# Two load queues instead of one: value loads of units 1 to 15 issued by ScalarE in a decode attention kernel

## The chip, the core and the metric

The kernel runs on one core of a Trainium2 chip. The metric is the device time of one execution in microseconds. The kernel before has a median of 440.01 us over 3 runs (439.67 to 440.44).

## What is computed

Two attention blocks, A and B, each decode one token for a batch of 4. Both have 32 query heads, 8 key/value heads, head size 128 and a cache of 8192 keys. Block A attends to all keys, block B to the last 2048 (`W`). The outputs lie side by side in one array of 4 x 1 x 1024.

```python
q = (x @ wq) -> (B, 32, 1, 128)          # x is 4 x 1 x 512
k, v = caches, each of 8 heads repeated 4 times
scores = einsum("bhqd,bhkd->bhqk", q, k) * 128 ** -0.5
p = softmax(scores)
out = einsum("bhqk,bhkd->bhqd", p, v) -> (B, 1, 4096) @ wo
# block A: keys 0..8191; block B: keys 6144..8191
```

The caches that are read are large and each value is used for one token only: 20 units, below, of 4 MiB of keys and 4 MiB of values, with 8 MiB of query weights and 8 MiB of output weights.

## The kernel before, in words

**Units and turns.** The work is cut into 20 units. Units 0 to 3 belong to block B: one batch element each, all 8 heads, 2048 keys. Units 4 to 19 belong to block A: two key/value heads of one batch element, all 8192 keys. Each unit has 4 MiB of keys (`K_sb`) and 4 MiB of values (`V_sb`), and each buffer has two slots, taken by even and odd units in turn. Two units make a turn; TensorE runs a hardware loop over ten turns, VectorE and ScalarE over the last seven (`emit_loop`), with the first three turns written out.

**TensorE, in one unit u.** Sixteen transpose jobs T0 to T15 (L279, four 128x128 transposes each of keys) go into four PSUM banks in rotation. Three jobs behind follow the scores S (L310). Even jobs are copied from PSUM to `KT_sb` by VectorE (L287), odd ones by ScalarE (L288). After the last transposes come the sums of the exponentials of unit u-1 (L338), a filler in even units or the output projection in odd ones (L384, `Wo_sb`), and 128 matmuls PV of probabilities and values of unit u-1 (L326). So unit u's keys are needed at its beginning, and its values only near the end of unit u+1.

**VectorE** finishes unit u-1 after PV with a small sum and a product (L489, L492); this last one is the event `otr`, and it frees the value slot of unit u-1. At the end of an odd unit VectorE adds the projection's result to `oacc` (L392), the event `ocp`. **ScalarE** has, per unit, eight copies L288 (jobs 1, 3, ... 15) and two exponentials (L457), in this order.

**Loads.** All large loads are issued by SyncE (SP), in one hand-written order: both query weights (into the value slots), keys of unit 0, and then for u = 1 to 20: keys of unit u, values of unit u-1, and in front of units 6, 8, ... 18 also a 1 MiB piece of the output weights `Wo_sb` for the turn that starts (behind the values of unit u-1). Block B's loads are four DMAs of 1 MiB each per unit and kind, block A's one of 4 MiB. The function is `kv_load`, and the helper that issues every DMA is at L568. What each waits for, in SP's own order, so that a later one never goes ahead of an earlier one that waits:

- keys of unit u: up to unit 5 the transposes of unit u-2 that free the slot; from unit 6 on `otr` of unit u-3, which comes at the end of unit u-2, after PV.
- values of unit u: `otr` of unit u-2, at the end of unit u-1.
- output weights of a turn: `ocp` of the turn before, at the end of its odd unit.

```python
w = [("otr", u - 2)] if kind == "V" else [("otr", u - 3)] if u >= 2 * T0P else [("T", tjob_idx[(u - 2, NJ - 1)])]
```

Block A's loads are preceded by a semaphore addition of 48 on the same engine, so that loads of 16 and of 4 x 16 counts look alike to the loops.

The values of unit 19 come in five pieces, followed by eight small pieces of output weights (`Wl_sb`), for a short end.

Of the kernel before, what the change touches and what calls it, by code (L numbers as in the profile page):

```python
# [14 lines left out]
def bass_concat_heads__gqa_block_cached__sliding_block_cached__decode_kernel(  # L15
# [16 lines left out]
    _, HKV, SK, DH = A_k_cache.shape  # L32
    HQ = A_wq.shape[1] // DH
    REP = HQ // HKV
    W = min(4096, max(256, SK // 4))
    assert DH == 128 and D % 128 == 0 and D <= 512
    DC = D // 128
    NT = SK // 64
    NSEG = 4
# [7 lines left out]
    NQP = 4  # L47
# [4 lines left out]
    NM = 128  # L52
    NBK = 4
    NFILL = 3
    NTH = NT // 2
    X = [A_x, B_x]
    KC = [A_k_cache, B_k_cache]
# [14 lines left out]
    with ExitStack() as es:  # L72
# [93 lines left out]
        def op(eng, fn, waits=(), inc=None, bump=None):  # L166
            waits = list(waits)
            if not (eng == "pe" and turn[0] is not None):
                waits = [w for w in waits if w is not None]
            t = turn[0] if eng == "pe" or (eng in ("dve", "act") and turn[0] is not None and turn[0] >= T0P) else None  # L170
            plan[eng].append(dict(fn=fn, waits=waits, inc=inc, turn=t, bump=bump))

        def add(d):
            op(d["eng"], d["fn"], waits=d["waits"], inc=d["inc"])
# [426 lines left out]
        assert pc == NC  # L601
        AFTER = {("S", 2): ("OT",), ("S", 5): ("OL",)}

        for u in range(NU):
            turn[0] = tn = u // 2
            odd = u % 2 == 0
            ev = {}
            extra = {}
            at = -1

            def anchored(d):
                extra.setdefault(at, []).append(d)
            for tok in TOK:
                if tok[0] == "T":
                    ev[tok[1]] = pe_T(u, tok[1])
                    if tok[1] % 2 == 0:
                        at = tok[1]
                elif tok[0] == "S":
                    pe_S(u, tok[1])
                elif tok[0] == "X":  # L620
                    if u % 2 == 1:
                        ev["opj"] = pe_job_OPJ(tn)
                    else:
                        pe_filler(NFILL)
                elif tok[0] == "SM":
                    pe_SM(u - 1)
                else:
                    pe_PV(u - 1, tok[1], waits=[("V", u - 1) if u >= 1 else None] if tok[1] == 0 else [])
                if odd and tok in AFTER:
                    kind = AFTER[tok][0]  # L630
                    anchored({"OT": pe_job_OT, "OL": pe_job_OL}[kind](tn))

            if u % 2 == 0 and tn:
                follow[opj_idx[tn - 1]] = tjob_idx[(u, 0)]
            for k in range(0, NJ, 2):
                add(ev[k])
                if k == 10:
                    add(dve_max(u, 0))
                for d in extra.get(k, []):
                    add(d)  # L640
            add(dve_max(u, 1))
            if units[u]["P"] == 0:
                add(dve_maxc(u))
            add(dve_addmask(u))
            if u >= 1:
                add(dve_sum(u - 1))
                add(dve_rcp(u - 1))
            add(dve_submask(u))
            add(dve_sub(u, 0))
            add(dve_sub(u, 1))  # L650
            if u >= 1:
                add_norm(u - 1)
            if u % 2 == 1:
                add(ev["opj"])

            for k in range(1, NJ, 2):
                add(ev[k])
            add(act_exp(u, 0, 1))
            add(act_exp(u, 1, 2))

            if u % 2 == 0:
                if tn:
                    op("pool", None, waits=[("ocp", tn - 1)])
                if tn - 1 == T0P + NSEG - 1:
                    op("pool", lambda pool: pool.tensor_copy(out=osb[:, 1, :], in_=oacc[:, :]), inc=("ocB", 0))
                    op("pool", lambda pool: pool.memset(oacc[:, :], 0.0), waits=[("ocB", 0)], inc=("ocB", 1))
                add(pool_otp(tn))
            if u + 1 < NU:
                add(pool_rq(u + 1))
            add(pool_ar1(u))  # L670
            if u >= 1 and units[u - 1]["P"] == 0:
                add(pool_oc(u - 1))
# [34 lines left out]
        op("act", lambda act: act.activation(out=osb[:, 0, H2:D], in_=halves[1], func=ACTF.Copy), waits=[("fin", 1)], inc=("Ef",))  # L707
        op("act", dma(out[:, 0, H2:D], osb[:, 0, H2:D]), waits=[("Ef",)], inc=("out", 2))

        def kv_load(kind, u):  # L710
            un = units[u]
            cache = (KC if kind == "K" else VC)[un["P"]]
            buf = K_sb if kind == "K" else V_sb
            slot = u % 2
            if kind == "K" and slot == 1 and u < L:
                op("sp", lambda sp: sp.sem_inc(sems["kh"], 16), bump=(sems["kh"], 16, ("KH", u)))
            if un["P"] == 1:
                for q in range(NSEG):
                    base = cache[un["b"], 2 * q, SK - W:SK, :]
                    src = bass.AP(tensor=base.tensor, offset=base.offset, ap=[[TS * DH, 64], [SK * DH, 2], [1, TS * DH]])  # L720
                    if kind == "K":
                        w = [("T", tjob_idx[(u - 2, 4 * q + 3)])] if u >= 2 else []
                    else:
                        w = [("otr", u - 2)] if u >= 2 else [("T", tjob_idx[(1, 1)])] if u else [("T", qp_idx[(1, NQP - 1)])]
                    op("sp", dma(buf[:, slot, q * TS:(q + 1) * TS, :], src), waits=w, inc=(kind if q == NSEG - 1 else kind + "h", u, q))
                return
            base = cache[un["b"], 2 * un["gp"], :, :]
            w = [("otr", u - 2)] if kind == "V" else [("otr", u - 3)] if u >= 2 * T0P else [("T", tjob_idx[(u - 2, NJ - 1)])]
            if kind == "V" and u == L:
                c0 = 0  # L730
                for i, n in enumerate(VCH):
                    t0, t1 = c0 * TC, (c0 + n) * TC
                    src = bass.AP(tensor=base.tensor, offset=base.offset + t0 * DH, ap=[[NT * DH, 128], [1, (t1 - t0) * DH]])
                    op("sp", dma(buf[:, slot, t0:t1, :].rearrange("p t d -> p (t d)"), src), waits=w, inc=("VL", i))
                    c0 += n
                return
            src = bass.AP(tensor=base.tensor, offset=base.offset, ap=[[NT * DH, 128], [1, NT * DH]])
            sem = sem_of((kind, u))
            op("sp", lambda sp: sp.sem_inc(sem, 48), waits=w, bump=(sem, 48, None))
            if kind == "K" and u == L:  # L740
                for h in range(2):
                    t0 = h * NTH
                    src = bass.AP(tensor=base.tensor, offset=base.offset + t0 * DH, ap=[[NT * DH, 128], [1, NTH * DH]])
                    op("sp", dma(buf[:, slot, t0:t0 + NTH, :].rearrange("p t d -> p (t d)"), src), inc=(kind, u, 0) if h == 0 else ("KH", u))
                return
            op("sp", dma(buf[:, slot, :, :].rearrange("p t d -> p (t d)"), src), inc=(kind, u, 0))

        for P in (1, 0):
            op("sp", dma(V_sb[:, 1 - P, :, :].rearrange("p t d -> p (t d)"), WQ[P].rearrange("(p c) n -> p (c n)", p=128)), inc=("WQ", P))
        kv_load("K", 0)  # L750
        for u in range(1, NU + 1):
            if u < NU:
                kv_load("K", u)
            kv_load("V", u - 1)
            tn = u // 2
            if u % 2 == 0 and tn in pieces:
                P, q = pieces[tn]
                src = WO[P][q * C * DH:(q + 1) * C * DH, :].rearrange("(p r) n -> p (r n)", p=128)
                op("sp", dma(Wo_sb[:, :, :].rearrange("p r n -> p (r n)"), src), waits=[("ocp", tn - 1)], inc=("wo", tn))
            if u == 16:  # L760
                op("sp", dma(out[:, 0, D:2 * D], osb[:, 1, :]), waits=[("ocB", 0)], inc=("out", 1))
# [14 lines left out]

        values = {}
        counters = {}
        for eng in plan:
            for o in plan[eng]:  # L780
                if o["bump"] is not None:
                    sem, amt, key = o["bump"]
                    counters[sem.name] = counters.get(sem.name, 0) + amt
                    if key is not None:
                        values[key] = (sem, counters[sem.name], amt)
                if o["inc"] is not None:
                    key = o["inc"]
                    sem = sem_of(key)
                    amt = 16 if key[0] in DMA_KEYS else 1
                    counters[sem.name] = counters.get(sem.name, 0) + amt  # L790
                    assert key not in values, key
                    values[key] = (sem, counters[sem.name], amt)
# [102 lines left out]

        @block.scalar
        def _(act):
            emit_loop("act", act, mybir.EngineType.Activation)

        @block.vector  # L900
        def _(dve):
# [33 lines left out]
```

## Time and profile before

| What | Value |
|---|---|
| Median of 3 runs | 440.01 us (439.67 to 440.44) |
| The profiled execution, its own time | 439.76 us |
| Its span in the trace | 437.9 us, so 1.9 us lie around it |
| Granted TensorE clock | 0.969 of full speed |
| Busy: TensorE, VectorE, ScalarE, GpSimd | 363.9, 209.5, 193.3, 29.1 us |
| Read from memory | 184.56 MB, 421 GB/s over the span |
| TensorE waits for block A's keys | 33.0 us, 10 times |

How to read it. The page has the busy time of each engine, the span in 40 slices with the DMA engines' share and rate, the DMA queues, and groups of instructions by line. A timeline lists an engine's instructions in order of time: start, busy time, engine, line, operation, and in square brackets the idle time before it with what ended it. The rows of SPq are the DMA issues of SyncE's instruction stream; POOLq and ACTq those of GpSimd and ScalarE. A row of DMA issues gives the count, the size of one, and the median time from issue to landing; asked for a short window, it gives this for a single load.

### The profile page before, as it was taken

The numbers are of one execution on the slowest core, as the hardware profiler recorded it, in microseconds if no ns is written. First come the engines' busy times: TensorE is split into PE (matmuls) and PEld (weight loads), VectorE is DVE, ScalarE is ACT, GpSimd is POOL, SyncE is SP. The second block draws the span as 40 slices with busy tenths as digits, with TensorE's granted clock in tenths as the row PEclk, the third lists the DMA queues.
The fourth block names the chain that finished last, engine by engine and source line by source line (L and its number), as shares of the span: only waits on it lengthen the run. The fifth ranks groups of instructions, "written<-read, shape, count | busy, mean of one in ns | idle before, by whom it ended". The sixth has DMA issues, their size and how long they took to land.

```text
span 437.9 us, 15510 instructions
## 1 busy us (share of the span) xinstructions
PE 363.9 (83%) x7174; PEld 336.5 (77%) x7184; DVE 209.5 (48%) x404; ACT 193.3 (44%) x217; POOL 29.1 (7%) x96
## 2 busy tenths in 40 slices
PE   0078898998998959896989598969878895989986
PEld 0068897997997959795979588968868795979975
DVE  0004455664565634463456247625644563556641
ACT  1033473563653625372635264534534361635630
POOL 7110000000000000000000000000100000000000
PEclk9999999999999997999899699989998999999999
DMA  8999999999999999999999999999999999999996
GB/s 336 431 412 418 419 419 419 421 445 406 450 431 431 417 445 431 434 428 431 434 434 428 432 434 431 428 434 431 406 456 431 431 428 434 431 431 410 446 407 253
DMA packets 12500, 184.75 MB, mean 422 GB/s; under 512 B 1428, under 2 KB 2504, under 8 KB 2760
## 3 DMA queue, kind: packets, MB, share of 16 engines
q1 hardware_dynamic: 12400, 184.56, 99.2%
q8 instruction: 8, 0.13, 0.1%
q14 instruction: 4, 0.03, 0.0%
q0 software_dynamic: 64, 0.02, 0.0%
q10 hardware_dynamic: 24, 0.01, 0.0%
HBM read 184.56 MB, written 0.01 MB: 421 GB/s over the span
## 4 chain that ended last, share of the span: by engine, by line
PE 51%; DMA 43%; issue 2%; DVE 1%; SPq 1%; PEld 1%; PEldq 0%
DMA K_sb<-in_A_k_cache_dram 29%; PE KT L279 25%; PE OT L326 10%; DMA K_sb<-in_B_k_cache_dram 7%; DMA V_sb<-in_A_v_cache_dram 7%; PE SB L310 4%; PE SA L310 4%; PE KT L384 4%; SPq L568 1%; PE SA L338 1%; DVE oacc L392 1%; PE KT L326 1%; PEld OT L326 1%; PE KT L262 0%; DVE OS L489 0%
## 5 line engine op out<-in xcount | busy, mean ns | idle before, releaser
L279 PE MATMUL KT<-identf,K_sb 128*128 128x128 f32 x1280 | 206.2, 294 | 44.0 <-DMA K_sb<-in_A_k_cache_dram 33.0
L288 ACT ACTIVATE KT_sb<-KT 128x1024 bf16<-128x1024 bf16 x160 | 163.4, 1025 | 121.1 <-PE KT L279 121.1
L279 PEld LDWEIGHTS KT<-identf,K_sb 128*128 128x128 f32 x1280 | 146.2, 148 | 49.4 <-DMA K_sb<-in_A_k_cache_dram 34.2
L287 DVE COPY KT_sb<-KT 128x512 int32<-128x512 int32 x160 | 110.5, 690 | 131.2 <-PE KT L279 129.9
L326 PE MATMUL OT<-PT,V_sb 128*128 128x64 bf16 x2560 | 78.1, 193 | 2.5 <-issue 1.4
L326 PEld LDWEIGHTS OT<-PT,V_sb 128*128 128x128 bf16 x2560 | 75.9, 98 | 2.7 <-issue 1.5
L457 ACT ACTIVATE PT<-Dt 128x512 bf16<-128x512 f32 x40 | 24.6, 632 | 84.1 <-DVE Dt L446 84.1
L310 PEld LDWEIGHTS SA<-RQc,KT_sb 128*128 128x128 bf16 x1280 | 56.7, 98 | 2.3
L310 PEld LDWEIGHTS SB<-RQc,KT_sb 128*128 128x128 bf16 x1280 | 51.1, 97 | 7.9 <-issue 4.4
L310 PE MATMUL SA<-RQc,KT_sb 128*128 128x16 bf16 x1280 | 56.2, 170 | 0.0
L310 PE MATMUL SB<-RQc,KT_sb 128*128 128x16 bf16 x1280 | 52.8, 170 | 0.0
L408 DVE TENSOR_REDUCE M<-SB 128x8 f32<-128x512 f32 (+1 forms) x20 | 13.8, 692 | 49.9 <-PE SB L310 49.9
L429 POOL PARTITION_ALL_REDUCE MB<-M1m x20 | 7.7, 387 | 333.3 <-DVE M1m L422 333.3
L384 PE MATMUL KT<-Wo_sb,OL 128*4 128x512 bf16 x80 | 18.9, 379 | 0.0
L200 PE MATMUL KT<-ident,x_sb 4*128 4x4 bf16 x8 | 0.6, 170 | 21.1 <-POOL identf L540 21.1
L200 PEld LDWEIGHTS KT<-ident,x_sb 4*128 4x128 bf16 x8 | 0.4, 113 | 21.3 <-issue 21.3
L464 DVE TENSOR_REDUCE LB<-SA 128x8 f32<-128x512 f32 (+1 forms) x20 | 13.7, 684 | 2.8 <-PE SA L338 2.8
L446 DVE TENSOR_TENSOR Dt<-SA,MBm 128x512 f32<-128x512 f32 x20 | 13.8, 692 | 0.7
L355 DVE TENSOR_TENSOR ORx<-KT,MSK 32x1024 bf16<-32x1024 bf16 x10 | 12.1, 1211 | 3.7 <-PE KT L350 3.7
L408 DVE TENSOR_REDUCE M<-SA 128x8 f32<-128x512 f32 (+1 forms) x20 | 13.6, 681 | 0.0
L446 DVE TENSOR_TENSOR Dt<-SB,MBm 128x512 f32<-128x512 f32 x20 | 13.6, 681 | 0.0
L338 PE MATMUL SA<-PT,onesb 128*128 128x128 bf16 x168 | 12.7, 218 | 0.0
(74 smaller groups left out, 119.7 us busy)
## 6 DMA issues: line engine op xcount, KB each, us to landing
K_sb<-in_A_k_cache_dram SPq DMA_DIRECT2D x15, 4096.0 KB, 22.6
V_sb<-in_A_v_cache_dram SPq DMA_DIRECT2D x15, 4096.0 KB, 30.6
K_sb<-in_B_k_cache_dram SPq DMA_DIRECT2D x16, 1024.0 KB, 22.0
V_sb<-in_B_v_cache_dram SPq DMA_DIRECT2D x16, 1024.0 KB, 18.4
V_sb<-in_B_wq_dram SPq DMA_DIRECT2D x1, 4096.0 KB, 12.5
V_sb<-in_A_wq_dram SPq DMA_DIRECT2D x1, 4096.0 KB, 22.0
Wo_sb<-in_B_wo_dram SPq DMA_DIRECT2D x4, 1024.0 KB, 11.9
K_sb<-in_A_k_cache_dram SPq DMA_DIRECT2D x2, 2048.0 KB, 18.9
```

The lines of the kernel that those rows point to most:

```text
L279: ins = pe.transpose(out=bkf[:, pi * 128:(pi + 1) * 128], in_=K_sbf[:, slot, t0:t0 + 2, :].rearrange("p t d -> p (t d)"), identity=identf[ ...
L287: return e.tensor_copy(out=KT_sb.bitcast(I32)[:, tj % NKT, :], in_=bkf.bitcast(I32)[:, :])
L288: return e.activation(out=KT_sb[:, tj % NKT, :], in_=bk[:, :], func=ACTF.Copy)
L310: ins = pe.matmul(out=stb[:, t % NTH * C:(t % NTH + 2) * C], lhsT=ktv[:, pi, :, e], rhs=RQc[:, u % 2, t // TS, e, :], start=(e == 0), stop ...
L326: ins = pe.matmul(out=otb[:, s * NW:s * NW + w], lhsT=V_sb[:, slot, t, :], rhs=PT[:, slot, t * C:t * C + w], start=(j == 0), stop=(j == n ...
L338: ins = pe.matmul(out=SA[u % 2][:, s * NM:(s + 1) * NM], lhsT=onesb[:, :], rhs=PT[:, u % 2, c0:c0 + NM], start=(i == 0), stop=(i == n - 1))
L355: return dve.tensor_tensor(out=ORx[:, :, :, :], in0=bk[0:NR, 0:128].rearrange("p (i o r) -> p r o i", o=1, r=C).broadcast_to([NR, C, C, 12 ...
L384: ins = pe.matmul(out=bk[0:Bn, 0:D], lhsT=OL[:, i, :], rhs=Wo_sb[:, i, :], start=(i == 0), stop=(i == C - 1))
L408: return dve.tensor_reduce(out=M1[:, h * n:(h + 1) * n].rearrange("p (s h) -> p s h", h=C), in_=bank[:, :].rearrange("p (s j h) -> p s h j ...
L446: return dve.tensor_tensor(out=Dt[:, h * NTH * C:(h + 1) * NTH * C].rearrange("p (s j h) -> p s j h", s=Sh, h=C), in0=bank[:, :].rearrange ...
L457: return act.activation(out=PT[:, u % 2, a:b], in_=Dt[:, a:b], func=ACTF.Exp, scale=scale)
L464: return dve.tensor_reduce(out=LB[:, 0:n].rearrange("p (s h) -> p s h", h=C), in_=SA[u % 2][:, 0:NSEG * NM].rearrange("p (s j h) -> p s h ...
```

## The change

The values of units 1 to 15 are issued by ScalarE, right after its first copy (job 1) of the same unit in its own instruction order; values of unit 0 and of units 16 to 19 stay with SP. In block B this is four DMAs of 1 MiB on ScalarE for units 1 to 3; in block A one addition of 48 and one DMA of 4 MiB for units 4 to 15. That makes 24 DMAs which leave SP's instruction stream and join ScalarE's. The wait of the values stays as it was (`otr` of unit u-2).

Because ScalarE's list is no longer the same in every turn, it is written out for all 20 units instead of being a loop over seven turns. SP can then wait on the semaphore of ScalarE's transpose jobs in every unit, and the keys' wait changes: from unit 6 on, keys of unit u wait for the last transpose of unit u-2 and no more for `otr` of unit u-3. The order of instructions on TensorE and VectorE is the same as before. The semaphore values of the value loads are counted by unit rather than by engine, since two engines now add to them.

```diff
+    VACT = range(1, 16)
...
-            t = turn[0] if eng == "pe" or (eng in ("dve", "act") and turn[0] is not None and turn[0] >= T0P) else None
+            t = turn[0] if eng == "pe" or (eng == "dve" and turn[0] is not None and turn[0] >= T0P) else None
...
+            q_eng = "act" if kind == "V" and u in VACT else "sp"
...
-                    op("sp", dma(buf[:, slot, q * TS:(q + 1) * TS, :], src), waits=w, inc=(kind if q == NSEG - 1 else kind + "h", u, q))
+                    op(q_eng, dma(buf[:, slot, q * TS:(q + 1) * TS, :], src), waits=w, inc=(kind if q == NSEG - 1 else kind + "h", u, q))
...
-            w = [("otr", u - 2)] if kind == "V" else [("otr", u - 3)] if u >= 2 * T0P else [("T", tjob_idx[(u - 2, NJ - 1)])]
+            w = [("otr", u - 2)] if kind == "V" else [("T", tjob_idx[(u - 2, NJ - 1)])]
...
-            op("sp", lambda sp: sp.sem_inc(sem, 48), waits=w, bump=(sem, 48, None))
+            op(q_eng, lambda e: e.sem_inc(sem, 48), waits=w, bump=(sem, 48, (kind + "b", u)))
...
-            op("sp", dma(buf[:, slot, :, :].rearrange("p t d -> p (t d)"), src), inc=(kind, u, 0))
+            op(q_eng, dma(buf[:, slot, :, :].rearrange("p t d -> p (t d)"), src), inc=(kind, u, 0))
...
             for k in range(1, NJ, 2):
                 add(ev[k])
+                if k == 1 and u in VACT:
+                    kv_load("V", u)
...
-            kv_load("V", u - 1)
+            if u - 1 not in VACT:
+                kv_load("V", u - 1)
...
-            emit_loop("act", act, mybir.EngineType.Activation)
+            emit("act", act)
```

## The prediction

> **What bounds the kernel now.** I read the page's slices first, then the DMA queues, TensorE's waits, and the timelines of SP, ScalarE and TensorE over one turn.
>
> ```profile
> DMA  8999999999999999999999999999999999999996
> ...
> q1 hardware_dynamic: 12400, 184.56, 99.2%
> ```
>
> The DMA engines are full from the first slice to the last but one, and nearly all is one queue, SP's. In the window 114 to 430 us the rate is 430 GB/s. So the kernel's time is the bytes of that queue; no change of order can take time away as long as the bytes stay, and a moment in which the queue runs dry is added to the end.
>
> ```profile
> PE KT L279 <- DMA K_sb<-in_A_k_cache_dram: 33.0, 10, 5.3
> ```
>
> TensorE is the faster partner: it waits for keys ten times. How far the loads are ahead of what TensorE lets SP issue shows in one turn (units 8 and 9) of SP's timeline:
>
> ```profile
> 185.05 0.33 SPq L568 DMA_DIRECT2D Wo_sb<-in_B_wo_dram  x1
> 185.56 0.33 SPq L568 DMA_DIRECT2D K_sb<-in_A_k_cache_dram  x1
> 185.98 0.37 SPq L568 DMA_DIRECT2D V_sb<-in_A_v_cache_dram  x1
> 202.55 0.33 SPq L568 DMA_DIRECT2D K_sb<-in_A_k_cache_dram  x1
> 202.98 0.38 SPq L568 DMA_DIRECT2D V_sb<-in_A_v_cache_dram  x1
> 225.69 0.33 SPq L568 DMA_DIRECT2D Wo_sb<-in_B_wo_dram  x1
> ```
>
> These are the output weights, keys 9, values 8, keys 10, values 9, and the next turn's weights. The same window's DMA view gives the time to landing:
>
> ```profile
> K_sb<-in_A_k_cache_dram SPq DMA_DIRECT2D x1, 4096.0 KB, 20.6
> V_sb<-in_A_v_cache_dram SPq DMA_DIRECT2D x1, 4096.0 KB, 29.9
> Wo_sb<-in_B_wo_dram SPq DMA_DIRECT2D x1, 1024.0 KB, 11.4
> ```
>
> So the weights land at 196.45, keys 9 at 206.16, values 8 at 215.88: 4 MiB take 9.7 us. Keys 10 and values 9 (23.0 and 32.3 us after their issue) land at 225.55 and 235.28, and the next weights, 12.1 us after issue, at 237.79: 1 MiB takes 2.5 us. When the weights are issued at 225.69, values 9 are still in transfer for another 235.28 - 225.69 = **9.6 us: this is the cover** that keeps the queue full. A turn is 2.5 + 4 x 9.7 = 41.3 us, and keys land just that far apart (206.16 and 247.5).
>
> **What the skill says.** The Trainium skill, "DMA: Bandwidth & Descriptors", section "Issuing engines are not separate DMA queues": loads issued by SP, ScalarE and GpSimd run on the same 16 DMA engines and interleave; another issuer saves only issue time. The trace agrees as far as it can: 99.2% of the engines' time is used by one issuer already, so there is nothing for a second one to fill. Same page, "Queues, rings and completion order": SP and ScalarE have a ring each on every engine, and an engine goes round robin between rings that have work. The trace shows the overtaking:
>
> ```profile
> MASKB<-MK POOLq DMA_DIRECT2D x2, 8.0 KB, 5.4
> ```
>
> These two were issued by GpSimd at about 22 us, when loads issued by SP before 7 us were still landing until 44 us; they landed after 5.4 us and not behind those 20 us. So a ring doesn't wait for the older loads of another ring. I take it that K and V loads will share the engines half and half.
>
> **The change, part by part.** *Issue time on SP*: 24 DMAs leave; SP waits most of the time, so this is worth nothing.
>
> *Issue time on ScalarE.* A block A load costs 0.37 us (above) plus the addition, about 0.5 us together, behind the first copy. In odd units that start after a stall ScalarE is idle for 0.68 us after that copy (207.36 + 1.02 to 209.07), which hides it. In even units the first two copies stand back to back:
>
> ```profile
> 186.52 2.03 ACT L288 ACTIVATE KT_sb<-KT 128x1024 bf16<-128x1024 bf16 x2 [2.27 <-PE KT L279]
> 188.87 1.02 ACT L288 ACTIVATE KT_sb<-KT 128x1024 bf16<-128x1024 bf16 x1 [0.33 <-PE KT L279]
> ```
>
> There up to 0.5 us goes to TensorE, which then waits for keys anyway: nothing. In units 1 to 3 four issues cost 2.5 us (SP's row "55.68 2.48" for values 1), the PSUM banks behind are not emptied, and TensorE is late by about 2.5 us each time, 7.5 us in sum. The cover there, at the weights' issue at 141.70, is 13.4 - 2.5 = 10.9 us, so 3.4 us remain: nothing, if the issue costs on ScalarE what it costs on SP. Unknown; bounds 0 and double (5 us per unit, 15 us, 4 us over the cover).
>
> *ScalarE's loop written out*: no copies added; more instructions to fetch, which the trace of before doesn't price; 0 to 2 us, I take 0, since it would have to hit the short stretches named below. It may also save the loop's turn, of which TensorE sees nothing.
>
> *The keys' earlier wait.* Even keys go at the end of T15 (196.40 in TensorE's timeline of unit 8) instead of after PV (202.03), 5.6 us earlier. Odd keys stay behind the weights in SP's order, which wait for `ocp` at the end of the odd unit before: no earlier. An earlier issue into a full ring brings nothing.
>
> *The values' later issue, and the sharing.* This is the cost. Before, values 9 were issued at 202.98, ahead of the landing of keys 9 (206.16). Now values 9 stand behind ScalarE's first copy of unit 9, so behind that landing. And values 8, which stood in line behind keys 9, now share the engines with them. Let x be the first transpose of an even unit (185.39). Weights and odd keys are issued at x - 0.3 and x + 0.2, even values after the first copy, at x + 2.3. If nothing older is left, these 2.5 + 9.7 + 9.7 = 21.9 us of work share the engines, and the odd keys with the weights ahead of them (12.2 us) end last. With 1.7 us from issue to full flow they land at x - 0.3 + 1.7 + 21.9 = x + 23.3, call it y (before: x + 20.8); TensorE, through with PV at x + 16.6, waits 6.7 us instead of 4.2. At y the work on hand is the even keys and the odd values, 19.4 us, and SP can issue nothing more before the weights' wait ends. How long is that? From the odd unit's first transpose to the weights' issue, in six turns of before: 20.2 (164.83 to 185.05), 19.5 (206.18 to 225.69), 19.8, 19.6, 19.6, 19.4; mean 19.7. Until bytes flow again it is 19.7 + 1.7 = 21.4 us. **So the queue is dry for 21.4 - 19.4 = 2.0 us in each turn**; the cover of 9.6 us was just the one value load that has now gone ahead.
>
> The 1.7: the same skill page, "Latency and other measured facts", gives 0.6 us from issue to first byte[...]; the first load of this kernel,
>
> ```profile
> V_sb<-in_B_wq_dram SPq DMA_DIRECT2D x1, 4096.0 KB, 12.5
> ```
>
> 12.5 - 9.7 = 2.8 us from issue to landing beyond the transfer, is the other end. The middle is 1.7. What counts against the sum: if even values start late enough behind packets of the other ring, one to two of their eight rounds (1.2 us each) are left at y, and cover as much. With a longer wait TensorE comes back slower (20.2 after its longest wait, 5.3 us): up to 0.5 more. So a turn costs 0 to 3.5 us.
>
> *Which turns.* At unit 6 cover is left (above). The queue runs dry at the ends of turns with units 7, 9, 11, 13, 15: five times. From unit 16 on values are SP's again, in the old order, and the end of the kernel is as before. **Sum: 5 x 2.0 = 10 us.** Against the profiled execution's own 439.76 (span 437.9 and 1.9 around it) that is 449.8, against the median 440.01 (0.25 above it) 450.0. I give 450.0.
>
> **Rivals.**
> 1. *No dry queue, not slower.* If the arbitration or the late start of the even values lets odd keys land with 2.0 us or more of values left, that remainder is the cover and the loop settles on the bytes: 440.0. For it: the balance is a difference of 21.4 and 19.4, and packets of 1.2 us are coarse. Against it: weights and keys are 12.2 us, the values 9.7, so the keys should end last.
> 2. *ScalarE as the brake.* If an issue costs ScalarE about double, TensorE is 15 us late after unit 3, the queue runs dry for 4 us at unit 6 as well, and in later turns 0.5 us of issue lengthens the odd unit five times: 450.0 + 4 + 2.5 = 456.5. For it: copies wait behind each issue. Against it: SP's rows show 0.33 to 0.6 us.
> 3. *Two rings pack better.* Block B's 1 MiB take 2.5 us where a quarter of 9.7 is 2.4; if two rings remove this on some 24 MiB, 1.5 to 2 us are gained, without dry turns: 438.3. Nothing in the profile speaks for it but this difference.
>
> **How the numbers follow.** Forecast (dry turns, 442 to 455): 0.62. ScalarE as brake (455 to 460): 0.20. No dry queue: 0.14, of which some ends just above. Better packing: 0.04. The likeliest is 450.0. The range is 441 to 459: below it lie the packing case and most of the exact no-change, above it only a doubled cost in full. A measurement can tell about 0.2% (0.9 us) from no change: faster 0.04, within 0.10, slower 0.86.
>
> **What would show it.** In the profile after: slices of the DMA row below full in five places about 43 us apart in the middle, the queue of ScalarE at some 63 MB (15 x 4.19); odd units (7, 9, ...) waiting 6 to 7 us for keys, even ones none; the weights of `Wo_sb` landing in 4 to 8 us (1.7 + 2.5, and what they share with the values) instead of 11.9, since nothing is ahead of them. Wrong would be: DMA row full throughout, or TensorE waiting in the values' line L326, or ScalarE's copies ending the waits of TensorE in block A.

## The result, and the profile after

The changed kernel takes 452.24 us (median of 6 runs, 451.15 to 454.03) against 439.78 us (6 runs) for the kernel before: 2.85% slower, ratio 1.0285, interval 1.0261 to 1.031. The profiled execution took 452.04 us with a span of 450.2, 12.3 us more than before in both. The page of the kernel after:

```profile
DMA  8999999999999999979998998999799979999996
GB/s 350 412 420 421 420 416 423 443 408 427 443 434 422 434 437 431 419 309 419 440 445 326 422 463 378 416 440 426 322 441 443 431 320 443 445 434 417 428 418 230
...
q1 hardware_dynamic: 8944, 121.64, 64.2%
q10 hardware_dynamic: 3480, 62.93, 32.7%
```

The bytes are the same 184.56 MB, now on two queues; q10 is ScalarE's. The rate has five dents (309, 326, 378, 322, 320); the kernel before moved 431 GB/s on the mean from 150 to 380 us, with no such dent. They lie at the ends of turns. In windows set around them (us, then busy time of each engine, granted clock, DMA share, GB/s), the kernel after shows:

```profile
core 0: us, PE busy (x) PEld busy (x) DVE busy (x) ACT busy (x) POOL busy (x), PEclk, DMA share, GB/s
191.70:196.00 4.30, 2.92 (x66) 2.72 (x61) 2.75 (x6) 1.47 (x3) 0.64 (x3) 1.00 0.26 74
237.20:239.00 1.80, 0.83 (x8) 0.83 (x9) 0.74 (x3) 0.00 (x0) 0.64 (x3) 1.00 0.36 46
280.80:282.10 1.30, 1.30 (x13) 1.15 (x12) 0.69 (x1) 0.33 (x1) 0.00 (x0) 1.00 0.50 158
323.20:325.40 2.20, 0.85 (x8) 0.85 (x9) 1.10 (x4) 0.24 (x1) 1.25 (x3) 1.00 0.26 45
366.90:369.60 2.70, 1.55 (x13) 1.41 (x14) 1.45 (x3) 0.42 (x2) 0.64 (x3) 1.00 0.30 64
```

The DMA share, the last figure but one, is 0.26 to 0.50 in all five. To see what each costs, the bytes of the DMA packets were counted in both traces, each packet's bytes spread evenly over its time, and the times were compared at which the same number had moved. Up to 191 us the kernel after is level (within 0.3 us). Then it falls behind by 3.5, 2.2, 1.1, 2.5 and 2.3 us, one step at each dent (means of the level stretches between them): 11.6 us in sum. The other 0.7 us of the 12.3 come after the last large load, at the output weights of the end; their cause stays open.

How a dent comes about, at the end of the turn of units 8 and 9. First the DMA view of the kernel after, for the short window in which the next turn's weights are issued, and then for that of the odd values (unit 9); the last figure is the time to landing:

```profile
Wo_sb<-in_B_wo_dram SPq DMA_DIRECT2D x1, 1024.0 KB, 4.7
```

```profile
V_sb<-in_A_v_cache_dram ACTq DMA_DIRECT2D x1, 4096.0 KB, 18.5
```

The weights, issued at 237.83, land after 4.7 us, where they needed 11 to 13 before: nothing was ahead of them. The values of unit 9, issued at 219.33, landed at 219.33 + 18.5 = 237.83. So the last load in line lands at the very moment in which SP issues the next one, and until bytes of that one flow the engines have nothing to move. The chain that leads there shows in three timelines of the kernel after, of SP, TensorE and ScalarE:

```profile
194.30 0.33 SPq L569 DMA_DIRECT2D Wo_sb<-in_B_wo_dram  x1
194.81 11.26 SPq L569 DMA_DIRECT2D K_sb<-in_A_k_cache_dram  x2
237.83 0.33 SPq L569 DMA_DIRECT2D Wo_sb<-in_B_wo_dram  x1
```

```profile
217.23 1.11 PE L280 MATMUL KT<-identf,K_sb 128*128 128x128 f32 x4 [5.96 <-DMA K_sb<-in_A_k_cache_dram]
```

```profile
195.76 1.02 ACT L289 ACTIVATE KT_sb<-KT 128x1024 bf16<-128x1024 bf16 x1 [2.27 <-PE KT L280]
195.85 0.33 ACTq L569 DMA_DIRECT2D V_sb<-in_A_v_cache_dram  x1
196.77 1.02 ACT L289 ACTIVATE KT_sb<-KT 128x1024 bf16<-128x1024 bf16 x1
```

The second row of SP is keys 9 and keys 10 (issued at 194.81 and 205.74). Between 206 and 237.8 SP issues nothing. TensorE waits 5.96 us for keys 9 (4.15 before), since values 8, issued at 195.85, went beside them. The third timeline shows something else: the load is issued 0.09 us after the copy begins, and the next copy follows without a gap. Here ScalarE's issue of a block A load costs its copies nothing.

### The profile page after: what moved, and what is told of

It is laid out like the page before. It is cut to its first block, busy times and chain, and to the rows that moved or that the text cites. A ratio compares the mean times of both kernels' runs of the same rounds, so it can differ in the third digit from the quotient of the medians.

```text
span 450.2 us, 15489 instructions
## 1 busy us (share of the span) xinstructions
PE 365.0 (81%) x7184; PEld 335.6 (75%) x7184; DVE 209.5 (47%) x404; ACT 193.0 (43%) x217; POOL 29.2 (6%) x96
## 3 DMA queue, kind: packets, MB, share of 16 engines
q10 hardware_dynamic: 3480, 62.93, 32.7%
HBM read 184.56 MB, written 0.01 MB: 410 GB/s over the span
## 4 chain that ended last, share of the span: by engine, by line
DMA 45%; PE 41%; PEld 6%; issue 2%; SPq 1%; ACT 1%; ACTq 1%; DVE 1%; PEldq 0%
DMA K_sb<-in_A_k_cache_dram 26%; PE KT L280 20%; PE OT L327 9%; DMA K_sb<-in_B_k_cache_dram 7%; DMA V_sb<-in_A_v_cache_dram 7%; DMA Wl_sb<-in_A_wo_dram 5%; PE SB L311 3%; PE SA L311 3%; PE KT L385 3%; PEld KT L280 2%; PEld OT L327 2%; SPq L569 1%; ACT KT_sb L289 1%; ACTq L569 1%; PEld SB L311 1%
## 5 line engine op out<-in xcount | busy, mean ns | idle before, releaser
L201 PE MATMUL KT<-ident,x_sb 4*128 4x4 bf16 x8 | 0.6, 170 | 20.2 <-POOL identf L541 20.2
## 6 DMA issues: line engine op xcount, KB each, us to landing
V_sb<-in_B_wq_dram SPq DMA_DIRECT2D x1, 4096.0 KB, 12.2
```

## The experiments

Twelve kernels, each against the kernel before on the same chip. The window of 150 to 380 us holds the turns of block A in which values may be on ScalarE; its DMA share and rate (the last two figures of a line of the view) tell whether the queues ran dry there. The line of the kernel before, and that of the kernel after:

```profile
150.00:380.00 230.00, 194.33 (x3723) 181.25 (x3728) 115.45 (x225) 104.54 (x111) 10.89 (x40) 0.94 1.00 431
150.00:380.00 230.00, 186.98 (x3538) 173.61 (x3537) 111.02 (x214) 100.14 (x106) 10.10 (x37) 0.92 0.96 409
```

| Run | Median us | Ratio and interval | Share, GB/s, 150 to 380 us |
|---|---|---|---|
| before | 439.7 | 1 | 1.00, 431 |
| the change | 452.24 | 1.0285 (1.0261 to 1.031) | 0.96, 409 |
| e1, no values on ScalarE | 439.89 | 1.0002 (0.9993 to 1.0011) | 1.00, 431 |
| e2, odd units | 458.38 | 1.042 (1.0403 to 1.0438) | see below |
| e3, even units | 454.28 | 1.0326 (1.0309 to 1.0343) | 0.94, 401 |
| e4, weights behind odd keys | 442.29 | 1.0063 (1.0046 to 1.0079) | 1.00, 431 |
| e5, block A only | 455.81 | 1.0365 (1.0348 to 1.0383) | 0.95, 403 |
| e6, units 1 to 9 | 446.26 | 1.0153 (1.0136 to 1.017) | 0.98, 421 |
| e7, short projection | 450.39 | 1.0244 (1.0223 to 1.0265) | 0.97, 412 |
| e8, long projection | 462.19 | 1.0514 (1.0497 to 1.0532) | 0.92, 393 |
| e9, odd units of block A | 441.7 | 1.0042 (1.0028 to 1.0056) | 1.00, 431 |
| e10, unit 3 alone | 456.79 | 1.0388 (1.0373 to 1.0404) | see below |
| e11, weights behind odd keys, units 1 to 11 | 439.88 | 1.0003 (0.9994 to 1.0011) | 1.00, 431 |
| e12, before with long projection | 441.27 | 1.004 (1.0025 to 1.0055) | 1.00, 431 |

The theory is that of the forecast: even values share the engines with odd keys and are gone when these land, and nothing can be issued until the odd unit ends, so the queue runs dry. Rivals: two rings are slower in themselves; ScalarE is a brake by its issues or its long list.

**e1: the written-out list and the keys' wait alone.**

```diff
-    VACT = range(1, 16)
+    VACT = range(0)
```

> No value load on ScalarE (VACT empty): ScalarE's list is still written out and even keys still go right after the last transposes. Dry queue theory: all loads are one queue in the old order, the cover of 9.6 us is back, so 440 (439 to 441). Rival ScalarE's written-out list (instruction fetch) costs: 443 or more. Rival that the earlier keys hurt: above 441.

439.89 us, ratio 1.0002. With the values on SP, ScalarE's written-out list and the keys' earlier wait cost nothing and bring nothing. But this run has its cover back, and a cover would hide a somewhat slower ScalarE (e12 shows how much it can hide). What ScalarE does where the cover is missing is read from the trace of the change. TensorE's waits there, from 150 to 380 us:

```profile
PE KT L280 <- DMA K_sb<-in_A_k_cache_dram: 36.1, 5, 10.9
PE KT L280 <- issue: 6.9, 5, 1.4
```

None is ended by ScalarE. From the first transpose of an odd unit to the weights' issue it is 20.1 us on the mean of five turns, where it was 19.7 before: whatever slows TensorE in these units, ScalarE's list, its issues or the clock, is at most 0.4 us of some 2.3 us lost in a turn. The rest of the loss is in where the values are issued.

**e2 and e3: half of the values each.**

```diff
-    VACT = range(1, 16)
+    VACT = range(1, 16, 2)
```

> Only the values of odd units (1, 3, ... 15) on ScalarE; values of even units stay on SP behind the odd keys. Dry queue theory: when odd keys land, the even values (9.7 us) are still in line behind them, beside even keys and odd values, so the cover is there: 439.5 to 441.5, five dry places gone. Rival sharing itself costs (two rings are slower than one): about half of the loss stays, 445 to 447. Rival ScalarE as brake: also about half, 445 to 447.

458.38 us: far off every expectation. The place is not where any theory had it. The page of e2:

```profile
DMA  9999999999993849999999999999999999999995
GB/s 368 392 423 420 420 420 417 425 448 415 442 416 156 325 181 460 414 460 414 414 460 402 454 431 414 460 414 428 445 414 452 417 413 461 414 440 414 440 412 188
```

One hole between 140 and 168 us, none later: in the window 209 to 376 us the share is 1.00 and the rate 431. Its trace's waits name the cause, and the DMA view of 90 to 93 us the load:

```profile
PEld OT L327 <- DMA V_sb<-in_B_v_cache_dram: 21.9, 1, 21.9
```

```profile
V_sb<-in_B_v_cache_dram ACTq DMA_DIRECT2D x4, 1024.0 KB, 34.1
```

The four pieces of values 3 have packets of 8 KB. Beside them SP's ring has block A's keys and values in packets of 32 KB. The pieces land at 106.7, 119.0, 131.2 and 143.0, each 12 us after the other where 2.5 us is their own time: one small packet goes for each large one (a piece has 8 packets on each of the 16 engines, and 8 x (0.31 + 1.21) = 12.2 us, the packets' durations in the trace). PV of unit 4 waits 21.9 us for them, and the queues run dry meanwhile. Whether that is all of e2 is settled by e9 and e10.

```diff
-    VACT = range(1, 16)
+    VACT = range(2, 16, 2)
```

> Only the values of even units (2, 4, ... 14) on ScalarE; values of odd units on SP, issued at the end of the even unit as before. Dry queue theory: the even values share with the odd keys and are gone when these land; even keys and odd values are 19.4 us against some 21 to the next weights, as in the full change: 448 to 453, the dry queue at the ends of turns 3 to 7. Rivals sharing or ScalarE as brake: half the loads there, half the loss, 445 to 447.

454.28 us, DMA share 0.94: the even values alone run the queue dry in the same five places, with steps of 3.5, 2.5, 3.2, 3.4 and 3.1 us, and 0.4 us at 150 us. That is more than in the full change and than I expected, in part because the profiled execution was a long one (456.34 us). Against both rivals: half of the loads cost at least as much as all of them. The odd units have no issue on ScalarE here, and from their first transpose to the weights' issue they took 20.2 to 20.7 us, no less than the 19.5 to 20.6 of the change.

**e4: the odd keys freed from the weights' wait.**

```diff
     for u in range(1, NU + 1):
         if u < NU:
             kv_load("K", u)
+        for args in late:
+            op(*args[0], **args[1])
+        late = []
...
-            op("sp", dma(Wo_sb...), waits=[("ocp", tn - 1)], inc=("wo", tn))
+            late.append((("sp", dma(Wo_sb...)), dict(waits=[("ocp", tn - 1)], inc=("wo", tn))))
```

> The full change, but on SP the 1 MiB of output weights of a turn stand behind the odd keys instead of ahead, so that odd keys go when the last transposes of the odd unit before are done, some 7 us ahead of the weights' wait. Dry queue theory: work is on hand at the end of the odd unit, 439.5 to 442. Rivals sharing or ScalarE as brake: nothing changes for them, 450 to 453.

442.29 us. All values of units 1 to 15 are on ScalarE as in the full change, and ten of the 12.5 us are gone. The page of e4 has no dent:

```profile
GB/s 334 429 416 418 421 417 422 421 449 430 407 441 429 435 420 444 438 435 407 453 429 429 417 441 429 429 421 447 432 423 438 432 432 429 435 435 412 444 403 171
```

So two rings move the bytes at the full rate, and the same issues on ScalarE cost nothing in these turns once something is left in line; the loss needs both the sharing and SP's wait. The 2.6 us that stay lie behind the last load: its bytes are all there at the same time as before, but TensorE reaches unit 19 at 412.1 instead of 408.0 (e11 takes this up).

**e5 and e6: other sets of units.**

```diff
-    VACT = range(1, 16)
+    VACT = range(4, 16)
```

> Values of units 4 to 15 on ScalarE, block B's (1 to 3, four issues each) on SP as before. Dry queue theory: block B's issues on ScalarE use up cover before unit 6 and no time, the five dry turns stay: 449 to 453, at most 1 us less than the full change. Rival ScalarE as brake: the 12 issues of units 1 to 3 are half of the issue time that was moved, so 3 us or more are gained: below 449.

455.81 us, against the expectation: with fewer loads on ScalarE the kernel is slower than the full change. Its window 150 to 380 us has 0.95, and there is a sixth dry place, at 150 to 154 us, 3.0 us. With block B's values on SP, values 4 share the engines with keys 5 as the later ones do; keys 5 land at 133.0 and TensorE waits 9.4 us in unit 5. In the full change values 4 stand behind the slow pieces of values 3 in ScalarE's ring (they land at 141.5), keys 5 are there at 118.3, and unit 6 is spared. ScalarE as brake is contradicted once more, and so is my reason why the turn of unit 6 was safe: in the full change it was spared by luck.

```diff
-    VACT = range(1, 16)
+    VACT = range(1, 10)
```

> Values of units 1 to 9 on ScalarE, of 10 to 19 on SP. Dry queue theory: turns with units 7 and 9 run dry, 3.3 and 2.1 us (as the first two places of the full change), the other three don't: 445 to 446.5. Rivals by number of loads: 18 of 24 issues are still on ScalarE, 9.3 of 12.5 us, 449; by bytes 9 of 15, 447.3.

446.26 us, as expected: two steps (4.5 and 1.3 us by the bytes), and from the turn in which values are SP's again none. (The steps of the full change that this and the next expectation name are within 0.2 us of those given above.)

**e7 and e8: the length of the odd unit.**

```diff
-                for i in range(C):
+                for i in range(1):
```

> The full change with one matmul instead of eight in the output projection of each turn (seven eighths of the projection of these turns are left out, all loads stay). The odd unit is shorter by 7 x 0.23 = 1.6 us on TensorE between the landing of odd keys and the weights' issue. Dry queue theory: each of five dry spells is 1.6 us shorter, but not below nothing (3.3, 2.1, 0.9, 2.4, 2.2 become 1.7, 0.5, 0, 0.8, 0.6): 443 to 446. Rivals sharing or ScalarE as brake: the time is set elsewhere, 450 to 453.

450.39 us: a miss. The odd unit did get shorter (217.48 to the weights at 235.71, 18.2 us instead of 20.6), but the loss fell by 1.8 us in sum and not by 6 to 9. From keys 9 to keys 15 three turns take 348.12 - 217.44 = 130.7 us, against 347.23 - 217.19 = 130.0 in the full change. The lengths now alternate: 44.1, 41.4, 45.2 us. In the long ones the even values end at the same time as the odd keys (261.74 and 261.56), in the short one 2.4 us later (305.39 and 302.96). In the full change they end 2.4, 2.4, 1.3 and 2.4 us later, and this rest, half of it their share, is a piece of cover that I had put at nothing. A shorter unit lets the weights go while odd values are still in transfer, even values start sooner beside them, and the rest is lost. This is read from landings; no run changes the rest by itself, so it is argued, not shown.

The trace shows a second reason why a shorter unit gains so little. In the turn of units 12 and 13 the weights were issued at 321.23, 2.8 us before values 13 landed (324.03), so by the forecast's sum this turn runs dry no more; it still lost 1.8 us. The first packets of the weights start at 322.9, 1.6 us after their issue; between 322 and 323 us the DMA share is 0.23, and the first 32 KB packets of the next values take up to 2.7 us where 1.21 is usual. So a cover that is only just there does not yet save the turn.

```diff
-                for i in range(C):
+                for i in range(2 * C):
...
-                    ins = pe.matmul(out=bk[0:Bn, 0:D], lhsT=OL[:, i, :], rhs=Wo_sb[:, i, :],
-                                    start=(i == 0), stop=(i == C - 1))
+                    ins = pe.matmul(out=bk[0:Bn, 0:D], lhsT=OL[:, i % C, :], rhs=Wo_sb[:, i % C, :],
+                                    start=(i == 0), stop=(i == 2 * C - 1))
```

> The full change with sixteen matmuls instead of eight in the output projection of each turn (the sum is taken twice). The odd unit is longer by 8 x 0.23 = 1.8 us. Dry queue theory: five dry spells longer by 1.8 us each, 452.2 + 9 = 459 to 463. Rivals sharing or ScalarE as brake: TensorE has slack, 452 to 454.

462.19 us, 10.0 more than the change, where 9 were expected. By the bytes, 8.4 us of this fall in the five dry turns (in a profiled execution that was 9.1 us longer than that of the change), so TensorE's 1.8 us per turn go to the end nearly in full; what remains comes after the last large load.

**e12: the same edit on the kernel before.** The edit is that of e8.

> The kernel before with sixteen matmuls instead of eight in each turn's output projection (the sum is taken twice). Its cover of 9.6 us takes 1.8 us per turn: no dry turn; only the last unit's end may be later by up to 1.8 us: 440 to 442, against some 10 us that the same edit cost in the full change.

441.27 us: 1.6 us for the last unit's end, and nothing for the other turns. The page's window shows 1.00 and 431. By the bytes this run is level with the kernel before until 430 us. Under the cover of 9.6 us TensorE's 1.8 us per turn are free; without the cover the same edit cost 10.0.

**e9 and e10: what was the matter with e2.**

```diff
-    VACT = range(1, 16)
+    VACT = range(5, 16, 2)
```

> Only values of units 5, 7, ... 15 on ScalarE, none of block B. Dry queue theory: as in the second half of the run with odd units 1 to 15, where no turn after unit 8 lost time, so 439.5 to 441.5. If odd values on ScalarE did cost in themselves (two rings, issue time): 444 or more.

441.7 us: the share is 1.00 in the whole window. Odd values of block A on ScalarE never run the queue dry, since the even values still stand behind the odd keys. The 2.0 us, a little over the expectation, are again behind the last load: keys 16 share with values 15, and TensorE starts unit 19 at 413.1 (408.0 before) in the profiled execution, a long one of 443.03 us.

```diff
-    VACT = range(1, 16)
+    VACT = range(3, 4)
```

> One value load alone on ScalarE, that of unit 3: four pieces of 1 MiB in packets of 8 KB, beside key and value loads of block A in packets of 32 KB on SP's ring. Theory of the uneven packets: one small packet for each large one, so 4 MiB take four times as long, land near 143 us and hold PV of unit 4 by some 20 us, as with all odd units on ScalarE: 454 to 459. If that loss came from the other odd units: 440.

456.79 us, as expected. One unit's values on ScalarE cost 17 us, more than all fifteen together. The four pieces:

```profile
V_sb<-in_B_v_cache_dram ACTq DMA_DIRECT2D x4, 1024.0 KB, 34.4
```

The last lands at 142.9, and PV of unit 4 waits 21.8 us. The packets can be counted: between the landings of the first and the second piece ScalarE's ring moved 127 packets of 8 KB and SP's 127 of 32 KB, between the second and the third 128 and 128. In the full change the same pieces end at 123.3, in time but for 0.5 us: values 4 stand behind them in ScalarE's ring there, instead of beside them in SP's as large packets.

**e11: both cures.** The edit of e4, and:

```diff
-    VACT = range(1, 16)
+    VACT = range(1, 12)
```

> Output weights behind the odd keys as in the fourth run, and values on ScalarE only up to unit 11. Theory: no dry turn, and with the last shared transfer well ahead of the end TensorE is on time in units 16 to 19: 439.5 to 440.6. If the 2.6 us of the fourth run came from the order of the weights (behind keys 19) and not from values 15 beside keys 16: 442 to 443 again.

439.88 us, ratio 1.0003: level with the kernel before. With the last shared load well ahead of the end, TensorE starts unit 19 at 408.8 (412.1 in e4, 408.0 before), so the 2.6 us of e4 came from the last shared loads and not from the order of the weights. No version beats the kernel before: its queue is full, and the bytes are the same in all.

## Why the prediction was right, point by point

- *The bound.* Right: in every run without dents the rate in the window is 431 GB/s, and the time is 439.9 to 442.3.
- *Nothing to gain from a second issuer.* Right: with values of eleven units on ScalarE and no dry turn, e11 is level with the kernel before, as the Trainium skill has it ("DMA: Bandwidth & Descriptors", section "Issuing engines are not separate DMA queues").
- *Packets of two rings alternate.* Right for equal packets: keys 9 and values 8, issued 1 us apart, took 22.4 and 23.8 us to land. What I did not draw from it: they alternate by packet and not by bytes, so 8 KB packets beside 32 KB ones get a fifth of the bytes. Value loads in packets of that kind occur in units 1 to 3 of the change, and TensorE waited only 0.5 and 1.4 us there (PV of units 4 and 5). That was luck: e10 shows what they can cost. (The output weights come in 8 KB packets too, 1 MiB in a turn.)
- *The odd keys land at x + 23.3.* Measured x + 22.6, 22.6, 23.9, 22.7; the wait of 6.7 us measured as 6.0, 6.0, 7.2, 6.1 (10.9 in unit 7).
- *19.7 us from there to the weights' issue.* Measured 20.6, 19.5, 19.8, 20.4, and 20.0 in unit 7.
- *1.7 us from issue to flow.* The weights issued at 237.83 have their first packets at 238.8 to 239.1: 1.0 to 1.2 us, within the two bounds of 0.6 and 2.8. But a restart cost more than this. The last value packets had ended at 237.1 to 237.4, some 0.5 us before their landing was signalled, and the first new packet on each engine took 0.8 to 1.2 us where 0.31 is usual for 8 KB. In the turns of units 9, 13 and 15 the weights were issued within 0.2 us of the last landing, and 2.2 to 2.5 us were lost: this is what the sum had at 1.7.
- *2.0 us in each of five turns.* Five places, with 3.5, 2.2, 1.1, 2.5, 2.3. The mean is 2.3, and part of this nearness is luck, since errors cancel. The restart is at least 0.5 us dearer and the odd units are longer by 0.4 us on the mean. Against this, the rest of even values at y, named as a counterweight and set to nothing, is there in four of the five turns: it lands 1.3 to 2.4 us after the odd keys, half of which is its own work, 0.6 to 1.2 us of cover. In the first place, the largest, the even values (168.7) land before the odd keys (174.3), and no rest is left. The sum of 10 was short by 1.6 us in the turns and 0.7 us at the end.
- *Block B's issues on ScalarE make TensorE 2.5 us late per unit.* Too high: counted from the first transpose of the unit, units 1, 2 and 3 end their transposes 1.0, 1.1 and 1.4 us later. *That unit 6 is safe for the cover left* was right in the outcome and wrong in the cause (e5), so that five turns ran dry, and not six, is luck.
- *The issue stands behind the whole first copy, at x + 2.3.* Wrong: it goes out 0.09 us after the copy begins, at x + 1.2. Little hung on it.
- *The signs.* They came as named: five dents 43 to 44 us apart, 62.93 MB on ScalarE's queue, waits for keys in odd units alone, and weights that land after 4.7 to 4.8 us at all five dents.
- *The rival without a dry queue* describes e4, e9 and e11, where something is left to transfer; the change itself has it not. *ScalarE as brake* falls by the waits of the change (at most 0.4 us in a turn, under e1), by e3 and by e5.

## What to carry to other kernels

In a kernel whose one load queue is always full, ask what is still in line when the slow wait of the issuer ends: here one 4 MiB load, 9.6 us, was the whole margin, and moving it to a second queue let it go early and be gone when it was needed. A second queue changes the order in which loads land, not the rate; check which transfer now lands last, which wait stands ahead of the next issue, and whether both queues use packets of the same size. Extra work on an engine with slack that costs next to nothing under a cover (e12: 1.6 us, all at the end) costs nearly its full length without one (e8: 10.0 us, 8.4 of them in the five turns). And the cover has to be longer than a restart, some 2 us here: in e7 a turn lost 1.8 us although a load was still in transfer when the next was issued.

## What the runs showed of the hardware

- Two queues shared the DMA engines packet by packet, both when their packets were equal (32 KB, the change) and when they were not: in e10 1 MiB in 8 KB packets landed every 12 us beside 32 KB packets, one small packet for each large one, and every 2.5 us alone.
- A load in ScalarE's list was issued while the copy ahead of it still ran (0.09 us after its start), and the next copy followed without a gap; four in a row (2.57 us) did hold the copies behind them, by 1.6 us of idle time.
- A queue that had run dry took 1.0 to 1.2 us from issue to bytes, and the first packets after it were slow: 0.8 to 1.2 us for 8 KB instead of 0.31 (the change, at 238.8), and up to 2.7 us for 32 KB instead of 1.21 (e7). In all, 2.2 to 2.5 us were lost where a load was issued as the last one landed.
